# Four of the sixteen x tiles turned by a transposing DMA instead of TensorE, and three steps of the MLP part put at a slot's end

## The chip, the cores and the metric

One core of a Trainium2 chip runs the whole kernel in one launch. The metric is the time of one execution on the device in microseconds (us), the median of several runs.

## The reference

The kernel computes one transformer block on x of 2048 rows by 512 columns, in float32:

```
h  = x + attention(layernorm(x) @ wqkv) @ wo
h2 = h + (relu(layernorm(h) @ w1 + b1) ** 2) @ w2 + b2
```

The attention has 32 heads of 16 columns each. A row looks at 8 positions: itself and those 2, 4, .. 14 rows before it, with softmax over the 8. The MLP is 1792 wide.

## The kernel before

**Tiles.** x is cut in 16 tiles of 128 rows. Matrix products on TensorE need the left operand turned, columns on partitions, so every tile of x (after its layernorm), of the attention's output o and of the normalised h is turned before its product. Each operand is held as a high and a low part in a reduced float format, and a product is three matmul groups, high by high, low by high and high by low, of four 128x512 matmuls each (`mm3`, L228). In the program's names `xh`, `xl` are the parts of x, `oh`, `ol` (or `ohl`) those of o, `w_h`, `w_l`, `big_h`, `big_l` those of weights or h.

**Two ways to turn a tile.** On TensorE (`transposes`, L201): four 128x128 transposes into PSUM (`tr`); ScalarE casts the high part (L152) and VectorE subtracts it for the low part (L155). By DMA: `turn_split` (L616, ScalarE) separates the upper and lower 16 bits of each value into two planes (`pl`), `turn_dma` (L620, SyncE) issues one `DMA_TRANSPOSE`, and `turn_join` (L625, ScalarE) puts the halves together again; casts follow as before. Before the change, all x tiles go by TensorE, and some tiles of o (the set `OV`) and of h (`HV`) by DMA.

**Stages.** The first phases, `first_phase(t0)` for t0 = 4, 6, .. 14, each compute the projections of two tiles, t0 and t0 + 1, in six products (`qkv_of`, tiles alternating, so the second product of a phase is the first that needs tile t0 + 1), and prepare the tiles of the next phase: load (L438), statistics (`x_stats`, L182 to L184 on ScalarE), normalisation (`x_norm`, L196), turn (`x_T`). Results go through PSUM copies (`y`, L523) to DRAM (L500), and the attention loads windows of k, v (L247) and q (L260) back. A phase has twelve half-slots m. `weight_job` (L573) loads and splits one piece of wo or w1. Then come three MLP units u = 0, 1, 2 over four tiles each and a last one, with `wo_product`, the addition of the residual and of b2 (`h_add`, `add_b2` L674 on POOL), and the split of w2 (`split_w2`).

**What sets the order.** The order of the program is written by hand, slot by slot. Steps are put on lists: `at(n, ...)` for the end of the slot n from now, `after(n, ...)` for the same place but behind the attention's steps. At the end of a slot:

```
    def end_slot(pe):
        now["pe"] += pe
        run(due)
        pump()
        run(amid)
        run(late)
        now["slot"] += 1
```

`run(due)` emits what `at` listed, `pump` emits attention steps (dots L339, sums L373, maximum and exponential L390 to L396, weighting L350 on VectorE and ScalarE; additions L407 on POOL) up to a modelled VectorE time, and `run(late)` emits what `after` listed. Every engine works through its instructions in that order and waits at each for what it needs. SyncE issues all DMAs, in order, so a load that waits for VectorE to free its buffer holds the DMAs behind it.

Of the kernel before, what the change touches and what calls it, by code (L numbers as in the profile page):

```python
# [9 lines left out]
F32R = mybir.dt.float32r  # L10
# [6 lines left out]
P = 128  # L17
KB = D // P
FB = F // P
R = 4  # L20
RI = 2
# [17 lines left out]
XT = (9, 11), (7, 8)  # L39
# [19 lines left out]
def block_kernel(ctx, tc, x, wqkv, wo, w1, b1, w2, b2, out):  # L59
# [42 lines left out]
    def row(name, shape=(P, D), dt=F32):  # L102
        return work.tile(list(shape), dt, name=name, tag="row", bufs=ROWS)
# [9 lines left out]
    def at(delta, fn, *a):  # L113
        due.setdefault(now["slot"] + delta, []).append((fn, a))

    def after(delta, fn, *a):
        late.setdefault(now["slot"] + delta, []).append((fn, a))
# [33 lines left out]
    def hi(dst, src):  # L151
        nc.scalar.copy(dst, src)  # L152
# [45 lines left out]
    def transposes(src, banks="tr"):  # L198
        tr = turn[banks].tile("tr").rearrange("p (k c) -> p k c", k=KB)
        for k in range(KB):  # L200
            nc.tensor.transpose(tr[:, k, :], src[:, k * P:(k + 1) * P], ident)  # L201
        now["pe"] += 0.44
        return tr

    def parts(tr, dst):
        n = len(dst)
        return [(dst[i], tr[:, i * KB // n:(i + 1) * KB // n]) for i in range(n)]

    def hi_T(tr, h_dst):
        for d, src in parts(tr, h_dst):  # L210
            hi(d, src)
# [220 lines left out]
    xt, xT = {}, {}  # L432
# [35 lines left out]
    def x_T(t):  # L468
        tr = transposes(xt.pop(t))
        xT[t] = row("xh", (P, KB, P), F32R), row("xl", (P, KB, P), F32R)  # L470
        at(0, hi_T, tr, [xT[t][0]])
        after(0, lo_T, tr, [xT[t][0]], [xT[t][1]])

    ny = [0]

    turn["mm"] = Turn("mm0", "mm1", "acc0", "acc1")
# [90 lines left out]
    jobs = [(wo_h, wo_l, wo, k, 0, D) for k in range(KB)]  # L567
# [37 lines left out]
    planes = {}  # L605
# [4 lines left out]
    def two_planes(a):  # L610
        return a.bitcast(U16).rearrange("p (two n) -> p two n", two=2)

    def turn_split(key, src):

        planes[key] = src, row("pl")
        nc.scalar.copy(two_planes(planes[key][1]), halves_of(src))  # L616
# [6 lines left out]
    def turn_join(key):  # L623
        src, pl = planes[key]
        nc.scalar.copy(halves_of(pl).rearrange("p two n -> p n two"),  # L625
                       two_planes(src).rearrange("p two n -> p n two"))
        planes[key] = pl.rearrange("p (k c) -> p k c", k=KB)
# [55 lines left out]
    def wo_product(t, slots):  # L683
        ps = turn["mm"].tile("wo")
        oh, ol = oT.pop(t)
        mm3(ps, lambda k: oh[:, k, :], lambda k: ol[:, k, :],
            lambda k: wo_h[:, k, :], lambda k: wo_l[:, k, :], lows_last=t in OV)
        for n, (fn, a) in zip(slots, ((h_add, (t, ps)), (h_norm, (t,)), (add_b2, (t,)),
                                      (spill, (t,)))):
            (after if fn in (h_norm, spill) else at)(n + (fn is add_b2), fn, *a)  # L690

# [283 lines left out]
    for n in range(16):  # L977
        gp, t = divmod(n, 4)
# [27 lines left out]

    def first_phase(t0):
        def chores(m):
            if t0 + 3 < 16:
                if m in (0, 2):  # L1010
                    at(0, x_stats, t0 + 2 + m // 2)

                early = t0 == 12
                if m + early in ((4, 6) if t0 == R else (6, 7)):
                    at(0, x_norm, t0 + 2 + (m + early) // 7 if t0 > R else t0 + m // 2)
                if m in XT[early]:
                    x_T(t0 + 2 + XT[early].index(m))
            if t0 + 5 < 16 and m in (6, 9):
                at(0, load_x, t0 + 2 + m // 3)
            if jobs and m % 3 == 0:  # L1020
                at(0, weight_job)
            k = t0 // 2 * 12 - 72 + m
            if k == 19:
                dve(HOLD)
            for t in range(R):
                if k == OT[t]:
                    at(0, load_h, t)
                    o_T(t)
                if t in HV and k == HK[t][0]:
                    at(0, h_split, t)  # L1030
                    after(0, turn_dma, ("h", t))
                if t in HV and k == HK[t][1]:
                    at(0, turn_join, ("h", t))
                if k == WO[t]:
                    wo_product(t, (1, 3, 4, 6))
                    now["pe"] += 2.73
                if k == HT[t]:
                    (at(0, h_parts, t) if t in HV else h_T(t))
            if k in W2:
                at(0, load_w2, W2.index(k))  # L1040

        def half(m):
            end_slot(1.37)
            chores(m)

        for n in range(6):
            chores(2 * n)
            qkv_of(t0 + n % 2, n // 2, lambda: half(2 * n + 1))
            end_slot(1.37)
# [40 lines left out]
    for u in range(R - 1):  # L1090
        now["sub"] = u
        first, end = u == 0, False
        fs = list(range(FB)) if first else [*sorted(place), 12, 13]
        fs += [f for f in range(12) if f not in fs and (u < 2 or f not in ENDS)]
        fs += ENDS if u == 2 else []
        need = [] if first else [f for f in fs if f < 12 and f not in place]
        acc = [psum.tile([P, D], F32, name="acc", tag=tag) for tag in ("acc0", "acc1", "tr0", "tr1")]
        js = range(R)


        todo, halves = {}, {}
        for i in js:
            t = R * (u + 1) + i
            if not end:
                a = i // 2 if u == 2 else 0
                o0 = OP[i] - a - (2 if i >= RI and t in OV else 0)
                if t in OV:
                    turned = [(o0, at, 0, o_split, t), (o0, at if i >= RI else after, i // RI, turn_dma, ("o", t)),
                              (o0 + 2, at, 0, o_join, t)]
                else:  # L1110
                    turned = [(o0, o_T, t)]
                if t in HV:
                    h0 = 11 + i
                    turned += [(h0, midway, 0, h_split, t), (h0, after, 0, turn_dma, ("h", t)),
                               (h0 + 2, at, 0, turn_join, ("h", t))]
                for p, *what in ((LH[i] - a, at, 0, load_h, t), *turned,
                                 (WP[i] - a, wo_product, t, (0, 1, 2 + 3 * a, 3 + 3 * a))):
                    todo.setdefault(p, []).append(what)
                p, h = (HP[i], i % 2) if u < 2 else HL[i]
                if t in HV:  # L1120
                    todo.setdefault(p, []).append((at, 0, h_parts, t))
                else:
                    (todo, halves)[h].setdefault(p, []).append((h_T, t))
            todo.setdefault(UP[i], []).append((at, 0, unspill, R * u + i))
        if u == 2:
            for p, *what in ((12, at, 0, t_load, 0), (12, at, 0, t_load, 1), (13, after, 0, t_sums, 0),
                             (13, after, 0, t_sums, 1), (13, at, 1, t_split, 0),
                             (14, after, 0, t_split, 1)):
                todo.setdefault(p, []).append(what)

        def half(p):
            run(due)
            for fn, *a in halves[p]:
                fn(*a)

        for p in range(FB + LAG):
            more = 0.0
            if p == FB:
                run(due)
                dve(HOLD)  # L1140
            if u < 2 and p == FB - 2:
                dve(HOLD)
            for fn, *a in sorted(todo.get(p, []), key=lambda x: x[0] is wo_product):
                fn(*a)
                more += 2.73 if fn is wo_product else 0.0
            if p < FB:
                mlp1(u, fs[p])
                more += 2.73
                if first:
                    at(0, split_w2, p)  # L1150
                    if p + 1 < FB:
                        load_w2(p + 1)
            q = p - LAG
            if q >= 0:
                f = fs[q]
                mlp2(u, f, acc, js, q == 0, q == FB - 1,
                     (lambda: half(p)) if p in halves else None)
                more += 2.74
                if f < 12 and (need or first and p < FB - LAG):
                    free.append(place.pop(f))  # L1160
                    if need:
                        at(1, fetch, need.pop(0))
            end_slot(more)
        for i in js:
            at(u // 2, finish, R * u + i, acc[i])
# [83 lines left out]
```

## Time and profile before

| | |
|---|---|
| runs | 510.28, 510.4, 510.7 us; median 510.4 |
| profiled execution | 510.82 us, of which the span is 509.0 us |
| TensorE (PE) busy | 498.7 us, 98% |
| VectorE (DVE) busy | 380.8 us, 75% |
| ScalarE (ACT) busy | 304.7 us, 60% |
| GpSimd (POOL) busy | 357.2 us, 70% |
| granted TensorE clock | 1.00 |

In the profile's lines PE is TensorE's matmuls, PEld its weight loads (beside them), DVE VectorE, ACT ScalarE, SP SyncE, which issues the DMAs. A timeline row has start and duration in us, engine, line, operation, output and inputs by the program's names, shapes, count, and in brackets the idle time before it with what ended that. Matmuls are pipelined: rows of one line overlap, and the time of a group is read from start to start. Of a group of rows the three numbers after the count are minimum, median and maximum in ns. "to landing" is the time from a DMA's issue until its data is there.

### The profile page before, as it was taken

What the parts mean: (1) busy time and instruction counts of PE and PEld (TensorE: products, weight loads), DVE (VectorE), ACT (ScalarE), POOL (GpSimd) and SP (SyncE); (2) the same over time, 40 slices, a digit from 0 to 9 for tenths busy, and PEclk for the clock granted to TensorE, in tenths of its full rate; (3) what the DMA queues carried; (4) which work ended last, traced back from release to release, by engine and by line L of the source; (5) the groups of instructions that cost most, each with busy time, mean ns of one, the idle gap of its engine ahead of it and who ended that gap; (6) DMA issues with size and microseconds to landing.
All of it is one profiled execution on the core that took longest, in us unless ns stands there. A gap on an engine that the chain in (4) does not pass through costs nothing.

```text
span 509.0 us, 7539 instructions
## 1 busy us (share of the span) xinstructions
PE 498.7 (98%) x2422; PEld 420.7 (83%) x2422; DVE 380.8 (75%) x512; ACT 304.7 (60%) x558; POOL 357.2 (70%) x434
## 2 busy tenths in 40 slices
PE   8999999999999999999999999989999999999997
PEld 7999778888888888887788888768888888998986
DVE  6469899999989799979879997898973137832233
ACT  4625677768346757386564566754556947566541
POOL 5714689986685899969777876976897465685610
PEclk9999999999999999999999999999999999999999
DMA  8577899989798898669676874967662372444212
GB/s 265 162 238 204 229 300 297 262 271 317 219 220 254 277 283 253 231 176 245 193 249 199 215 195 130 263 221 231 210 160 67 102 217 82 166 127 142 64 42 82
DMA packets 109359, 102.61 MB, mean 202 GB/s; under 512 B 29448, under 2 KB 77832, under 8 KB 109320
## 3 DMA queue, kind: packets, MB, share of 16 engines
q1 hardware_dynamic: 108376, 101.61, 68.0%
q10 hardware_dynamic: 944, 0.52, 0.3%
q8 instruction: 19, 0.31, 0.3%
q14 instruction: 20, 0.16, 0.1%
HBM read 72.65 MB, written 24.25 MB: 190 GB/s over the span
## 4 chain that ended last, share of the span: by engine, by line
PE 41%; POOL 5%; ACT 4%; DMA 3%; DVE 1%; issue 1%; SPq 0%; POOLq 0%; DVEq 0%; ACTq 0%
PE acc L895 19%; PE mm L228 12%; PE mm L818 6%; PE wo L228 3%; POOL pr L407 2%; DMA o<-pl 1%; DMA hn<-pl 1%; POOL h L674 1%; DMA h<-h_d 1%; ACT pl L625 1%; ACT pl L616 1%; ACT hn L196 1%; DVE pr L350 0%; POOL o L407 0%; PE tr L201 0%
## 5 line engine op out<-in xcount | busy, mean ns | idle before, releaser
L407 POOL TENSOR_TENSOR pr<-pr 128x512 f32<-128x512 f32 (+1 forms) x128 | 133.7, 1044 | 34.6 <-DVE pr L350 29.1
L228 PE MATMUL mm<-big_l,w_h 128*128 128x512 f32 x336 | 88.5, 390 | 1.6 <-DVE big_l L155 0.9
L350 DVE TENSOR_TENSOR pr<-ex,v 128x1024 f32<-128x1024 f32 x64 | 78.1, 1221 | 13.1 <-POOL o L407 8.1
L339 DVE TENSOR_TENSOR pr<-qp,k 128x1024 f32<-128x1024 f32 x64 | 76.8, 1200 | 8.8 <-ACT qp L268 6.9
L373 DVE TENSOR_REDUCE ex<-pr 128x64 f32<-128x1024 f32 x64 | 78.5, 1226 | 1.9
L228 PEld LDWEIGHTS mm<-big_l,w_h 128*128 128x128 f32 x336 | 62.9, 188 | 15.4 <-issue 1.3
L155 POOL TENSOR_TENSOR rl<-r,rh 128x512 fp32r<-128x512 f32 x42 | 55.5, 1322 | 20.2 <-ACT rh L152 20.2
L228 PE MATMUL mm<-big_l,xh 128*128 128x512 f32 (+1 forms) x208 | 55.8, 378 | 0.0
L228 PE MATMUL mm<-big_h,xh 128*128 128x512 f32 (+1 forms) x208 | 53.9, 380 | 1.3 <-ACT xh L152 1.0
L228 PE MATMUL mm<-big_h,xl 128*128 128x512 f32 (+1 forms) x208 | 52.7, 375 | 0.7 <-DVE xl L155 0.7
L895 PE MATMUL acc<-big_l,rh 128*128 128x512 f32 x190 | 52.2, 390 | 0.0
L895 PE MATMUL acc<-big_h,rh 128*128 128x512 f32 x190 | 52.1, 391 | 0.0
L895 PE MATMUL acc<-big_h,rl 128*128 128x512 f32 x190 | 51.7, 389 | 0.0
L228 PEld LDWEIGHTS mm<-big_h,xh 128*128 128x128 f32 x208 | 37.6, 188 | 8.9 <-ACT xh L152 2.6
L228 PE MATMUL mm<-big_l,w_l 128*128 128x512 f32 x168 | 44.9, 389 | 0.0
L228 PEld LDWEIGHTS mm<-big_h,xl 128*128 128x128 f32 x208 | 38.2, 188 | 6.9 <-DVE xl L155 1.1
L871 ACT ACTIVATE r<-mm,b_sb 128x512 f32<-128x512 f32 x42 | 28.7, 684 | 22.5 <-PE mm L228 20.7
L895 PEld LDWEIGHTS acc<-big_h,rl 128*128 128x128 f32 x190 | 35.7, 188 | 7.4
L895 PEld LDWEIGHTS acc<-big_l,rh 128*128 128x128 f32 x190 | 35.5, 188 | 7.4
L228 PEld LDWEIGHTS mm<-big_l,xh 128*128 128x128 f32 x208 | 37.5, 188 | 4.9
L895 PEld LDWEIGHTS acc<-big_h,rh 128*128 128x128 f32 x190 | 34.9, 188 | 6.7
L228 PEld LDWEIGHTS mm<-big_l,w_l 128*128 128x128 f32 x168 | 31.5, 188 | 6.6
(167 smaller groups left out, 918.7 us busy)
## 6 DMA issues: line engine op xcount, KB each, us to landing
k<-qkv_d SPq DMA_DIRECT2D x48, 288.0 KB, 3.0
v<-qkv_d SPq DMA_DIRECT2D x48, 288.0 KB, 4.1
qkv_d<-y SPq DMA_DIRECT2D x18, 512.0 KB, 4.7
big_l<-w2l_d SPq DMA_DIRECT2D x24, 256.0 KB, 3.0
xt<-in_A_x_dram SPq DMA_DIRECT2D x16, 256.0 KB, 4.2
q<-qkv_d SPq DMA_DIRECT2D x32, 128.0 KB, 3.8
h<-in_A_x_dram SPq DMA_DIRECT2D x16, 256.0 KB, 4.2
h_d<-h SPq DMA_DIRECT2D x16, 256.0 KB, 3.2
```

Of the source, the lines that this page charges most:

```text
L155: eng.tensor_tensor(out=dst, in0=src, in1=h, op=ALU.subtract)
L196: nc.scalar.activation(dst, src, AF.Identity, scale=rs[:, 0:1], bias=rs[:, 1:2])
L228: nc.tensor.matmul(ps, l(k), r(k), start=(n == 0), stop=(n == 3 * KB - 1))
L339: nc.vector.tensor_tensor(out=pr.rearrange("p i w h d -> p i w (h d)"), in0=qps["now"][:, j % 2].unsqueeze(2).to_broadcast([P, RI, W, GC]) ...
L350: nc.vector.tensor_tensor(out=p2, in1=vwin, op=ALU.mult, in0=e1[:, :, :, j * GH:(j + 1) * GH].unsqueeze(4).to_broadcast([P, RI, W, GH, DH]))
L373: nc.vector.tensor_reduce(out=lf[:, :, :, j * GH:(j + 1) * GH], in_=pr, axis=X, op=ALU.add)
L407: nc.gpsimd.tensor_tensor(out=dst, in0=p2[:, :, :w], in1=p2[:, :, w:2 * w], op=ALU.add)
L616: nc.scalar.copy(two_planes(planes[key][1]), halves_of(src))
L625: nc.scalar.copy(halves_of(pl).rearrange("p two n -> p n two"), two_planes(src).rearrange("p two n -> p n two"))
L818: nc.tensor.matmul(ps, sta[y][:, k], mov[x][:, k], start=(first and q == 0), stop=(last and q == len(terms) - 1), skip_group_check=True)
L871: nc.scalar.activation(r, ps, AF.Relu, bias=b1_sb[:, f:f + 1])
L895: nc.tensor.matmul(acc[j], l[:, j * P:(j + 1) * P], w[f], start=(first and n < len(js)), stop=(last and n >= len(terms) - len(js)))
```

## The change

Tiles 9, 11, 13 and 15, each the second of its phase's pair, are turned by DMA. `x_split` is listed at half-slot 8 of the phase before (7 for tile 15), with its DMA at the end of that slot; `x_join` stands at half-slot 0 of the tile's own phase, ahead of the next tiles' statistics (tile 15: at half-slot 11 of the phase before its own). `x_T` stays for the first tile of a pair, and for both tiles of the first of these phases. The weight jobs' half-slots change in the phases. In the MLP part the addition of b2, the split of w2, and the split and DMA of the third attention tile of a unit (`i == RI`) move from `at` to `after`.

```
+    def x_split(t):
+        turn_split(("x", t), xt.pop(t))
+
+    def x_join(t):
+        turn_join(("x", t))
+        tr = planes.pop(("x", t))
+        xT[t] = row("xh", (P, KB, P), F32R), row("xl", (P, KB, P), F32R)
+        hi_T(tr, [xT[t][0]])
+        after(0, lo_T, tr, [xT[t][0]], [xT[t][1]])
...
-            (after if fn in (h_norm, spill) else at)(n + (fn is add_b2), fn, *a)
+            (at if fn is h_add else after)(n + (fn is add_b2), fn, *a)
...
+            if m == 0 and 6 < t0 < 14:
+                at(0, x_join, t0 + 1)
+            if m == 11 and early:
+                at(0, x_join, 15)
...
-                if m in XT[early]:
+                if m in XT[early][:1 + (t0 == R)]:
                     x_T(t0 + 2 + XT[early].index(m))
+                if t0 > R and m == 8 - early:
+                    at(0, x_split, t0 + 3)
+                    after(0, turn_dma, ("x", t0 + 3))
...
-            if jobs and m % 3 == 0:
+            if jobs and m in ((0, 3, 6, 9) if t0 < 8 else (0, 4, 8) if t0 < 14 else (0, 3, 5)):
                 at(0, weight_job)
...
-                    turned = [(o0, at, 0, o_split, t), (o0, at if i >= RI else after, i // RI, turn_dma, ("o", t)),
+                    turned = [(o0, after if i == RI else at, 0, o_split, t),
+                              (o0, at if i > RI else after, i // (RI + 1), turn_dma, ("o", t)),
                               (o0 + 2, at, 0, o_join, t)]
...
-                    at(0, split_w2, p)
+                    after(0, split_w2, p)
```

On SyncE at the end of the phase t0 = 6, where tile 9 is turned (`xt` are x tiles, `qkv_d` the stored projections, `y` their copies, `raw` pieces of weights, `pl` the planes), the rows of before and then of after:

```order
54 L500 DMA qkv_d<-y_90 128x8x128
55 L247 DMA k<-qkv_d 128x704
56 L260 DMA q<-qkv_d 128x2x128
57 L438 DMA xt<-in_A_x_dram 128x512
58 L573 DMA raw<-in_B_w_dram 128x448
```
```order
54 L510 DMA qkv_d<-y_90 128x8x128
55 L247 DMA k<-qkv_d 128x704
56 L260 DMA q<-qkv_d 128x2x128
57 L630 DMA_TRANSPOSE xt<-pl 128x8x128
58 L438 DMA xt<-in_A_x_dram 128x512
59 L583 DMA raw<-in_B_w_dram 128x448
```

The transpose stands behind the k and q loads, and the xt load and the weight load move one place back. The lines of the changed kernel are 10 higher here.

On ScalarE at the turn of that phase to t0 = 8 (L196 the normalisation, L152 casts, L182 to L184 statistics, L268 the copy of q for the attention, L396 the exponential, `y` a result's copy out of PSUM), before and after:

```order
79 L152 CAST w_h<-raw 128x448
80 L152 CAST xh<-tr 128x512
81 L523 COPY y_90<-mm 128x8x64
82 L152 CAST xh<-tr 128x512
83 L152 CAST w_h<-raw 128x448
84 L523 COPY y_90<-mm 128x8x64
85 L182 ACTIVATE scrap,nm<-xt 128x512
86 L183 ACTIVATE nm<-nm 128x1
87 L184 ACTIVATE scrap,sq<-xt,nm 128x512
88 L268 COPY qp<-q 128x256
89 L523 COPY y_90<-mm 128x8x64
```
```order
78 L626 COPY pl<-xt 128x1024
79 L396 ACTIVATE ex<-ex 128x128
80 L152 CAST w_h<-raw 128x448
81 L152 CAST xh<-tr 128x512
82 L533 COPY y_90<-mm 128x8x64
83 L152 CAST w_h<-raw 128x448
84 L533 COPY y_90<-mm 128x8x64
85 L635 COPY pl<-xt 128x1024
86 L152 CAST xh<-pl 128x512
87 L182 ACTIVATE scrap,nm<-xt 128x512
88 L183 ACTIVATE nm<-nm 128x1
89 L184 ACTIVATE scrap,sq<-xt,nm 128x512
```

The second cast of x from PSUM is gone; the split stands ahead of an exponential, and the join with its cast stands between a result's copy and the statistics of the next tiles.

On ScalarE in the MLP unit u = 0, around the third attention tile's split (L871, L872 the squared relu and `rh` its high part, `hn` the normalised h), before and after:

```order
230 L152 CAST rh<-r 128x512
231 L616 COPY pl<-o 128x1024
232 L152 CAST big_h<-raw_2434 128x512
233 L396 ACTIVATE ex<-ex 128x256
234 L196 ACTIVATE hn<-h,rs 128x512
235 L871 ACTIVATE r<-mm,b_sb 128x512
```
```order
237 L152 CAST rh<-r 128x512
238 L268 COPY qp<-q 128x256
239 L396 ACTIVATE ex<-ex 128x256
240 L196 ACTIVATE hn<-h,rs 128x512
241 L626 COPY pl<-o 128x1024
242 L152 CAST big_h<-raw_2422 128x512
243 L881 ACTIVATE r<-mm,b_sb 128x512
```

The split of o and that of w2 stand behind the exponential and the normalisation, where they stood ahead of them.

More of the change, by code (lines that the diff above doesn't have):

```diff
@@ L1008, in chores @@
         def chores(m):
+            early = t0 == 12
+            if m == 0 and 6 < t0 < 14:
+                at(0, x_join, t0 + 1)
+            if m == 11 and early:
+                at(0, x_join, 15)
             if t0 + 3 < 16:
@@ L1011, in chores @@
                     at(0, x_stats, t0 + 2 + m // 2)
-                early = t0 == 12
                 if m + early in ((4, 6) if t0 == R else (6, 7)):
                     at(0, x_norm, t0 + 2 + (m + early) // 7 if t0 > R else t0 + m // 2)
-                if m in XT[early]:
+                if m in XT[early][:1 + (t0 == R)]:
                     x_T(t0 + 2 + XT[early].index(m))
+                if t0 > R and m == 8 - early:
+                    at(0, x_split, t0 + 3)
+                    after(0, turn_dma, ("x", t0 + 3))
             if t0 + 5 < 16 and m in (6, 9):
                 at(0, load_x, t0 + 2 + m // 3)
-            if jobs and m % 3 == 0:
+            if jobs and m in ((0, 3, 6, 9) if t0 < 8 else (0, 4, 8) if t0 < 14 else (0, 3, 5)):
                 at(0, weight_job)
```

## The prediction

> **What bounds the kernel now.** I read the page first (span, busy shares), then the busy time by stretches through the stage in which the x tiles are turned, then the timelines of TensorE, SyncE and ScalarE around the four places that lose transposes, and last the idle times of TensorE in the MLP part.
>
> ```profile
> span 509.0 us, 7539 instructions
> PE 498.7 (98%) x2422; PEld 420.7 (83%) x2422; DVE 380.8 (75%) x512; ACT 304.7 (60%) x558; POOL 357.2 (70%) x434
> DMA  8577899989798898669676874967662372444212
> 75.00:90.00 15.00, 15.00 (x72) 12.40 (x71) 14.47 (x24) 10.85 (x27) 13.86 (x19) 1.00 0.98 302
> 90.00:105.00 15.00, 15.00 (x72) 12.40 (x71) 14.53 (x20) 10.62 (x25) 13.41 (x19) 1.00 0.92 274
> 105.00:120.00 15.00, 15.00 (x72) 12.40 (x71) 13.95 (x18) 10.25 (x23) 13.86 (x20) 1.00 0.88 279
> ```
>
> TensorE is busy for 498.7 of 509.0 us. The row of digits is the busy share of the DMA engines in 40 slices of 12.7 us, in tenths: it is highest up to slice 16 (203 us) and lower after it. In the stretches of 15 us (columns: PE, PEld, DVE, ACT, POOL busy, granted clock, share of the DMA engines, GB/s) it is busy the whole time at clock 1.00, so a TensorE instruction taken out there shortens the span by its time, and a TensorE wait put in there lengthens it. Two other columns bear on the change: DVE is 14 of 15 us busy, so what holds DVE is not caught up within a phase, and the DMA engines are 88 to 98% busy, so a transfer put there queues.
>
> **The transposes that go.** Sixteen TensorE transposes are removed, four for each of tiles 9, 11, 13 and 15.
>
> ```profile
> 77.40 1.09 PE L228 MATMUL mm<-big_h,xh 128*128 128x512 f32 x4
> 78.79 0.60 PE L201 MATMUL tr<-ident,xt 128*128 128x128 f32 x4
> 80.62 1.07 PE L228 MATMUL mm<-big_h,xh 128*128 128x512 f32 x4
> 83.34 1.07 PE L228 MATMUL mm<-big_h,xh 128*128 128x512 f32 x4
> ```
>
> The product that holds tile 9's transposes (78.79) runs from 77.40 to 80.62, 3.22 us; the next, without, from 80.62 to 83.34, 2.72 us. One tile's transposes so cost 0.50 us of TensorE, and four tiles 4 x 0.50 = **-2.0 us**. [...]
>
> **Where the turned tile now comes from.** In the new path ScalarE splits the normalised tile into two planes, SyncE issues one transposing DMA, ScalarE joins the planes and casts the high part, and VectorE forms the low part. Each step stands in order on its engine: behind the join on ScalarE are the statistics, the query copy and the next result's copy; behind the low part on VectorE is the attention. The pieces that the trace has:
>
> ```profile
> 78.92 0.47 SPq L260 DMA_DIRECT2D q<-qkv_d  x1
> 79.48 0.46 SPq L438 DMA_DIRECT2D xt<-in_A_x_dram  x1
> 85.14 0.63 ACT L182 ACTIVATE scrap<-xt 128x512 f32<-128x512 f32 x1 [0.39 <-DMA xt<-in_A_x_dram]
> L625 ACT COPY pl<-o x12: 1163/1174/1178, 199.0 to 405.5; 128x1024 uint16<-128x1024 uint16 x12
> L152 ACT CAST oh<-pl x9: 620/621/628, 200.2 to 406.8; 128x512 fp32r<-128x512 f32 x9
> L620 SPq DMA_TRANSPOSE o<-pl x12: 1237/1242/3462, 195.4 to 395.8; - x12
> DMA to landing us min/median/max: 3.6/4.4/7.0
> ```
>
> *Tile 9.* On SyncE the new transpose stands where this xt load stands at 79.48, directly behind the query load of 78.92, so it can go no earlier than about 79.4 whatever ScalarE does: the key load ahead of it waits for VectorE to free its buffer. The xt load issued there landed at 85.14 (ScalarE's statistics were released by it then), 5.7 us after issue; the transposes of the trace, issued where DMA is less busy, landed after 3.6 to 7.0 us. I take 85.1, the same place in the queue and the same bytes (128x512 in float32, two 128x512 planes of 16 bits). Then join 1.17 and cast 0.62 give the high part at 85.14 + 1.79 = 86.93. TensorE wants it at the first product of tile 9, which was at 83.34 and would be at 82.84 without the 0.50 us of transposes. The stall is 86.93 - 82.84 = **4.1 us**. Bounds: a landing 3.6 us after 79.4 gives 83.0 + 1.79 = 84.8 and 2.0 us; 7.0 us gives 86.4 + 1.79 = 88.2 and 5.4 us. Nothing gets ahead meanwhile: ScalarE stands at the join until 85.1, VectorE at the low part until 86.9, SyncE's loads wait for VectorE's buffers. So the 4.1 us are paid in full and the stages behind move by about the same.
>
> ```profile
> 95.41 0.32 SPq L247 DMA_DIRECT2D v<-qkv_d  x1
> 95.82 0.38 SPq L438 DMA_DIRECT2D xt<-in_A_x_dram  x1
> DMA to landing us min/median/max: 4.2/4.2/4.2
> 100.62 1.07 PE L228 MATMUL mm<-big_h,xh 128*128 128x512 f32 x4
> 110.12 0.43 SPq L500 DMA_DIRECT2D qkv_d<-y  x1
> 117.91 1.07 PE L228 MATMUL mm<-big_h,xh 128*128 128x512 f32 x4
> 129.13 0.33 SPq L247 DMA_DIRECT2D v<-qkv_d  x1
> 145.26 1.07 PE L228 MATMUL mm<-big_h,xh 128*128 128x512 f32 x4
> ```
>
> *Tile 11* (times as before, the earlier stall left out, since all move together). Its transpose stands behind the value load of 95.41, where an xt load is issued at 95.82 and lands 4.2 us later (the landing shown is that load's alone). 95.8 + 4.2 + 1.79 = 101.8 against a need at 100.62 - 0.50 = 100.12: **1.7 us** (3.6 us: 1.1; 7.0 us: 4.5). *Tile 13.* Issue behind the store of 110.12, at 110.6; even with 5.0 us to landing the high part is there at 117.4, and it is wanted at 117.91 - 0.50 = 117.41: 0 (7.0 us: 2.0). *Tile 15.* Issued behind the load of 129.13, joined four half-slots later, wanted around 145.26: 0 at any landing of the trace. Sum of stalls **5.8 us**, between 3.1 and 11.9.
>
> [...]
>
> The other edits of this stage cost nothing that I can find: X in phases where ScalarE is 10 to 11 of 15 us busy, and as many weight jobs as before remain, spread otherwise over the slots.
>
> **The MLP part.** Here TensorE does wait a little:
>
> ```profile
> 234.22 1.20 PE L228 MATMUL mm<-big_l,w_h 128*128 128x512 f32 x4 [0.69 <-ACT r L871]
> 250.81 0.66 PE L201 MATMUL tr<-ident,hn 128*128 128x128 f32 x4 [0.69 <-ACT hn L196]
> 321.39 1.20 PE L228 MATMUL wo<-wo_h,ohl 128*128 128x512 f32 x4 [0.54 <-ACT ohl L152]
> 332.25 1.20 PE L228 MATMUL wo<-wo_h,ol 128*128 128x512 f32 x4 [0.44 <-DVE ol L155]
> 343.47 1.15 PE L228 MATMUL mm<-big_l,w_h 128*128 128x512 f32 x4 [0.93 <-DVE big_l L155]
> 218.44 1.05 ACT L616 COPY pl<-o 128x1024 uint16<-128x1024 uint16 x1 [7.07 <-POOL o L407]
> 219.40 0.61 ACT L152 CAST big_h<-raw 128x512 fp32r<-128x512 f32 x1
> 220.31 0.42 DVE L362 TENSOR_REDUCE sm<-ex 128x32 f32<-128x256 f32 x1 [3.10 <-ACT ex L396]
> 309.15 1.05 ACT L616 COPY pl<-o 128x1024 uint16<-128x1024 uint16 x1 [7.46 <-POOL o L407]
> 310.50 0.42 DVE L362 TENSOR_REDUCE sm<-ex 128x32 f32<-128x256 f32 x1 [2.76 <-ACT ex L396]
> 224.25 1.25 SPq L620 DMA_TRANSPOSE o<-pl  x1
> 230.42 1.32 POOL L674 TENSOR_TENSOR h<-h,b_sb 128x512 f32<-128x512 f32 x1
> 231.67 1.78 POOL L155 TENSOR_TENSOR rl<-r,rh 128x512 fp32r<-128x512 f32 x1
> ```
>
> The five waits are 0.69 + 0.69 + 0.54 + 0.44 + 0.93 = 3.29 us. The third attention split holds ScalarE 7 us waiting for POOL, and the exponential queued behind it comes late for VectorE by 3.10 and 2.76 us. Put behind the exponential and the normalisation, it holds neither; its DMA, at 224.25 though the planes were ready about 219.5, moves ahead of a key load that waits. The bias addition (1.32 us) moves behind the low part of r, which comes that much earlier. I count the three waits directly on these chains (234.22, 321.39, 332.25: 1.67 us) as gone, and half of the other two (0.81): **-2.5 us**, from 0 (the turned tile or another result is next by as much) to -3.3. The weight split at a slot's end leaves ScalarE's later work free sooner and I count nothing for it. If the idle time of ScalarE that covers it is gone, its cast (0.61 us at 219.40) would come into the wait for r once per weight block.
>
> **The sum.** -2.0 + 5.8 - 2.5 = +1.3 us. The profiled execution took 510.82 us, 509.0 of it span; it would become 512.1. The runs shown have a median of 510.4, 0.4 below it, so the time is 510.4 + 1.3 = **511.7 us**. What a measurement here can tell from no change is about 0.2%, 1.0 us: 511.7 is just beyond it.
>
> **Rivals.** *A, early landings, faster.* If the transposes of tiles 9 and 11 land at the fast end, 3.6 us, the stalls are 2.0 + 1.1 = 3.1, and with all 3.3 us of the MLP waits gone it is -2.0 + 3.1 - 3.3 = -2.2: 508.2 us. It turns faster by over 1.0 us where the stalls are under 3.5 with 2.5 recovered. For it: the fast transposes of the trace. Against: those ran with DMA less busy, while here it is 98%, and the load in that very place took 5.7. *B, late landings, slower by more.* At 7.0 us for tiles 9 and 11 the stalls are 5.4 + 4.5 = 9.9; with 2.0 recovered, -2.0 + 9.9 - 2.0 = +5.9: 516.3. For it: the slowest transpose of the trace took that where DMA was less busy than here; against: the load's 4.2 at tile 11. *C, nothing recovered.* The stalls of the forecast come, and in the MLP the waits stay, since the attention's end there is set by POOL, which ended both splits' waits: -2.0 + 5.8 = +3.8: 514.2. *D, a wash.* The transposes wait for nothing and hide, and the MLP waits stay but for one: it needs landings under 2 us at tile 9, which no row shows, or stalls near 4.5 with 2.5 recovered: 510.4.
>
> **How the numbers follow.** The forecast's own case (stalls 4.5 to 7, half or more recovered) has 0.45, of which about 0.10 falls within 0.2%; A 0.18, all faster; B 0.17; C 0.13; D 0.07, same. Faster 0.19, same 0.17, slower 0.64. The range runs from A, 508.2, to somewhat over B, 517.0 (B with 1.3 recovered), which leaves about one in ten outside on either side.
>
> **What would show it.** In the new trace: no transposes of xt near 78.8, 96.1, 113.4, 130.2; a TensorE wait on the high part of x in front of tile 9's first product of about 4 us and in front of tile 11's of about 2, none for 13 and 15; ScalarE's join released by the DMA there; VectorE idle for the high part at the same places. In the MLP, the 3.10 and 2.76 us idle times of VectorE gone and TensorE's waits under 1 us in sum. A TensorE that runs through tile 9's start without a wait would make the forecast wrong, and so would a wait for tile 13.

## The result, and the profile after

The changed kernel takes 521.88 us (median of four runs, 521.43 to 523.0) against 510.34 before: a ratio of 1.0231, 95% interval [1.0211, 1.0251]. It is 11.5 us slower. The forecast was 511.7 us in a range of 508.2 to 517.0: the direction was right and the size was not.

The page of the changed kernel, its span, busy times and DMA row, and the same three stretches as before:

```profile
span 519.9 us, 7521 instructions
PE 502.3 (97%) x2406; PEld 421.8 (81%) x2406; DVE 375.1 (72%) x512; ACT 312.8 (60%) x566; POOL 355.5 (68%) x434
DMA  9677989789798888958577766785754373255212
75.00:90.00 15.00, 11.25 (x42) 8.63 (x41) 12.20 (x18) 9.55 (x22) 10.50 (x15) 0.82 1.00 283
90.00:105.00 15.00, 15.00 (x66) 12.33 (x65) 11.80 (x17) 8.25 (x18) 11.71 (x15) 0.95 0.70 193
105.00:120.00 15.00, 13.95 (x63) 11.17 (x63) 11.86 (x17) 12.64 (x27) 10.24 (x15) 1.00 0.81 247
```

Two things stand out. TensorE waits in the stretches where it never did, and although it has 16 instructions fewer it is busy 3.6 us longer: in the first stretch the granted clock is 0.82 in the mean. The rows of TensorE around the four tiles and in the MLP part of the changed kernel:

```profile
79.25 1.07 PE L228 MATMUL mm<-big_h,xh 128*128 128x512 f32 x4
86.04 2.07 PE L228 MATMUL mm<-big_h,xh 128*128 128x512 f32 x4 [3.75 <-ACT xh L152]
87.91 1.91 PE L228 MATMUL mm<-big_l,xh 128*128 128x512 f32 x4
89.62 1.91 PE L228 MATMUL mm<-big_h,xl 128*128 128x512 f32 x4
91.33 1.17 PE L228 MATMUL mm<-big_h,xh 128*128 128x512 f32 x4
106.72 1.21 PE L228 MATMUL mm<-big_h,xh 128*128 128x512 f32 x4 [1.05 <-ACT xh L152]
124.53 1.19 PE L228 MATMUL mm<-big_h,xh 128*128 128x512 f32 x4 [0.66 <-ACT xh L152]
...
240.55 1.20 PE L228 MATMUL wo<-wo_h,ohl 128*128 128x512 f32 x4 [2.15 <-ACT ohl L152]
241.59 1.82 PE L228 MATMUL wo<-wo_l,ohl 128*128 128x512 f32 x4
243.82 1.77 PE L228 MATMUL wo<-wo_h,ohl 128*128 128x512 f32 x4 [0.41 <-DVE ohl L155]
245.42 1.09 PE L228 MATMUL mm<-big_l,w_h 128*128 128x512 f32 x4
```

Tile 9's product starts 3.75 us late and then takes 91.33 - 86.04 = 5.29 us where one takes 2.72, since every group of four matmuls takes nearly twice its time (2.07, 1.91 and 1.91 us against 1.07; the granted clock is 0.50 from 86 to 90 us). The same happens after the wait of 2.15 us at 240.55 (0.50 from 242 to 244 us): that product takes 4.87 us, 0.41 of it a second wait.

TensorE's first turn of h in the MLP part, before and after:

```profile
157.51 0.60 PE L201 MATMUL tr<-ident,hn 128*128 128x128 f32 x4
163.81 0.60 PE L201 MATMUL tr<-ident,hn 128*128 128x128 f32 x4
```

So TensorE leaves the first phases 6.3 us late: -0.9 from smaller waits in the first 70 us, -2.0 from the transposes, +5.5 from the three waits, +2.6 from the slow product, and 1.1 that I can't assign row by row. In the MLP part, from this row to the last matmul (it starts at 505.40 before and 516.56 after), 4.9 us more are lost: the waits there add up to 6.3 us where they were 3.3, and the slow product at 240 us costs 1.7. The remainder of the span gives 0.3 back.

ScalarE and SyncE at tile 9, the steps of which the forecast's stall was made:

```profile
77.78 0.32 SPq L247 DMA_DIRECT2D k<-qkv_d  x1
78.16 0.48 SPq L260 DMA_DIRECT2D q<-qkv_d  x1
78.73 1.52 SPq L630 DMA_TRANSPOSE xt<-pl  x1
84.12 1.16 ACT L635 COPY pl<-xt 128x1024 uint16<-128x1024 uint16 x1 [4.08 <-DMA xt<-pl]
85.37 0.62 ACT L152 CAST xh<-pl 128x512 fp32r<-128x512 f32 x1
```

The transpose stands behind the two loads, lands 5.4 us after its issue, and join and cast follow at once, as forecast.

### The profile page after: what moved, and what is told of

Read it like the earlier page. It is cut to its first block, busy times and chain, and to the rows that moved or that the text cites. A ratio compares the mean times of both kernels' runs of the same rounds, so it can differ in the third digit from the quotient of the medians.

```text
span 519.9 us, 7521 instructions
## 1 busy us (share of the span) xinstructions
PE 502.3 (97%) x2406; PEld 421.8 (81%) x2406; DVE 375.1 (72%) x512; ACT 312.8 (60%) x566; POOL 355.5 (68%) x434
## 4 chain that ended last, share of the span: by engine, by line
PE 37%; POOL 8%; ACT 6%; DVE 5%; issue 3%; POOLq 0%; DVEq 0%; ACTq 0%
PE acc L905 16%; PE mm L228 11%; PE mm L828 6%; POOL pr L407 4%; PE wo L228 3%; DVE pr L350 2%; ACT pl L626 1%; POOL rl L155 1%; POOL o L407 1%; ACT r L881 1%; ACT pl L635 1%; ACT r L882 1%; ACT hn L196 1%; DVE ol L155 1%; POOL h L684 0%
## 5 line engine op out<-in xcount | busy, mean ns | idle before, releaser
L350 DVE TENSOR_TENSOR pr<-ex,v 128x1024 f32<-128x1024 f32 x64 | 78.0, 1220 | 14.3 <-POOL o L407 9.9
L228 PE MATMUL mm<-big_h,xh 128*128 128x512 f32 (+1 forms) x208 | 55.0, 386 | 6.2 <-ACT xh L152 6.1
```

Of the source, the lines that this page charges most:

```text
L228: nc.tensor.matmul(ps, l(k), r(k), start=(n == 0), stop=(n == 3 * KB - 1))
L350: nc.vector.tensor_tensor(out=p2, in1=vwin, op=ALU.mult, in0=e1[:, :, :, j * GH:(j + 1) * GH].unsqueeze(4).to_broadcast([P, RI, W, GH, DH]))
```

## The experiments

The questions were whether the MLP loss is the price of the late attention (theory 1) or of the MLP edits (theory 2), and what the slow clock costs.

**All x tiles on TensorE again** (the cadence of the weight jobs and the MLP edits stay):

```
-            if m == 0 and 6 < t0 < 14:
-                at(0, x_join, t0 + 1)
-            if m == 11 and early:
-                at(0, x_join, 15)
...
-                if m in XT[early][:1 + (t0 == R)]:
+                if m in XT[early]:
...
-                if t0 > R and m == 8 - early:
-                    at(0, x_split, t0 + 3)
-                    after(0, turn_dma, ("x", t0 + 3))
```

> All x tiles are turned on TensorE again; the new weight cadence and the MLP edits stay. Theory 1 (the MLP part is slow after the change because the attention comes out of the first phases late; its own edits are harmless): TensorE's waits in the MLP are back to 3.3 us or less in sum, the clock is 1.00 throughout, and the time is 508 to 511 us. Theory 2 (the MLP edits themselves cost the 4.9 us): the stalls at tiles 9, 11, 13 and the slow clock there are gone, but the waits near 240 us stay, and the time is 510.4 + 5 = 515 us.

Measured: 509.07 us, ratio to before 0.9987 [0.9971, 1.0002]. The MLP edits with the new cadence cost nothing; whether they gain 0.1% can't be told. Theory 2 falls.

**The MLP edits undone**, the turned tiles kept (the three lines of the diff on `add_b2`, the third split and `split_w2` as before):

> The MLP edits are undone (bias addition, third split and its DMA, weight split at their old places); the turned x tiles and the cadence stay. Theory 1: the late attention still meets the MLP part: 520 to 525 us. Theory 2: the MLP part is as before, the loss is that of the first phases alone (+6.3 us in the trace): 516 to 517 us.

Measured: 521.09 us, 1.0233 [1.0197, 1.0269]. Most of the loss in the MLP part stays without the edits: in the trace TensorE leaves the first phases at 164.53, 7.0 us late, and the MLP part is 2.9 us longer than before, where it was 4.9 with the edits. Nothing here speaks against theory 1 yet.

**Tile 9 alone on TensorE:**

```
-            if m == 0 and 6 < t0 < 14:
+            if m == 0 and 8 < t0 < 14:
...
-                if m in XT[early][:1 + (t0 == R)]:
+                if m in XT[early][:1 + (t0 <= 6)]:
...
-                if t0 > R and m == 8 - early:
+                if t0 > 6 and m == 8 - early:
```

> Tile 9 alone is turned on TensorE again. Both theories: the 3.75 us stall and the slow clock behind it (2.9 us) go, 0.5 us of transposes come back, so TensorE leaves the first phases about 6.1 us earlier. Theory 1: with the attention less late, the MLP loss of 4.9 us shrinks to 2 or less: 511 to 513 us. Theory 2: it stays: 515 to 516 us.

Measured: 512.94 us, 1.006 [1.0042, 1.0078], 8.9 us less than the changed kernel. The time came where theory 1 had it, but not in its way. TensorE leaves the first phases at 160.80, 3.0 us earlier than in the changed kernel and not 6.1, since tile 11 now waits 2.00 us and its product runs slow (the granted clock is 0.997 in the mean of the span, 1.00 before). The MLP loss is gone altogether: that part is 0.4 us shorter than before, though TensorE comes to it 3.3 us late.

**TensorE kept busy in the wait:**

```
+            if t0 == 8 and n == 1:
+                keep_busy(16)
             qkv_of(t0 + n % 2, n // 2, lambda: half(2 * n + 1))
```

> Sixteen matmuls that nothing uses (3.6 us of TensorE at full clock) stand between the first product of tile 8 and the first of tile 9, in the wait. If the clock falls because TensorE stands idle, the granted clock stays 1.00 from 84 to 92 us, tile 9's first product takes 2.7 us and not 5.3, and the time is 521.9 - 2.6 = 519.3 us or lower. If it falls for another reason (DMA load, power at that place), the time stays near 522 us.

Measured: 523.3 us, 1.0261 [1.0236, 1.0286]. TensorE's rows of this kernel, and stretches of its time:

```profile
82.94 3.79 PE L1020 MATMUL tr<-big_h 128*128 128x512 f32 x16
87.20 1.20 PE L228 MATMUL mm<-big_h,xh 128*128 128x512 f32 x4 [0.47 <-ACT xh L152]
88.24 1.08 PE L228 MATMUL mm<-big_l,xh 128*128 128x512 f32 x4
107.82 1.20 PE L228 MATMUL mm<-big_h,xh 128*128 128x512 f32 x4 [3.51 <-ACT xh L152]
84.00:88.00 4.00, 3.53 (x16) 2.60 (x15) 1.46 (x3) 2.61 (x5) 1.95 (x3) 1.00 1.05 336
88.00:92.00 4.00, 4.00 (x19) 3.31 (x18) 2.93 (x6) 3.90 (x13) 1.42 (x5) 1.00 0.58 186
```

Half of the expectation came: the clock stays at 1.00 from 84 to 92 us, where the changed kernel has 0.58 from 84 to 88 and 0.56 from 88 to 92, and tile 9's product takes 2.86 us (the next one starts at 90.06). With the DMA engines as busy as in the changed kernel (a share of 1.05 here, 1.02 there, from 84 to 88 us) and a wait of 0.47 us in place of 3.75, it was TensorE's standing idle that took the clock down here. The time doesn't follow: tile 11's wait grows from 1.05 to 3.51 us. What tile 11 waits for is its own chain, a transpose behind a value load that waits for VectorE (1.3 us in the changed kernel, for L390), then the landing (5.1 us there), join and cast; that chain had lost its time at tile 9 and takes no notice of how fast TensorE ran in between. The slow product was hidden under a wait to come.

**The x tiles' DMA one step earlier** (`at` in place of `after`, so that it stands ahead of the key or value load):

> The x tiles' transposing DMAs are listed with at, so that each stands ahead of the key or value load that it stood behind: tile 9's can start when its planes are ready, about 76.1 us, where it started at 78.7. Theory 1 (the wait is the transfer's start and landing, and what VectorE loses in it is not regained): about 2.5 us earlier at tile 9 and up to as much at tile 11, less lag of the attention and most of the MLP loss gone: 512 to 516 us. Theory 3 (DMA is saturated there and the landing moves little whatever the issue): 520 to 522 us.

Measured: 516.29 us, 1.0131 [1.0104, 1.0159], 5.6 us less than the changed kernel. The start of the transfer matters; theory 3 falls. But its MLP part still shows the 2.15 us wait, and TensorE leaves the first phases 0.3 us ahead of before. The lateness was gone and the loss in the MLP part, 5.7 us, was not.

**Normalisation and split three half-slots earlier:**

```
+                elif m in (4, 6):
+                    at(0, x_norm, t0 + 3 if m == 4 else t0 + 2)
...
-                if t0 > R and m == 8 - early:
+                if t0 > R and m == (7 if early else 5):
```

> In the phases of t0 = 6, 8 and 10 the second tile is normalised at half-slot 4 (was 7) and split at 5 (was 8), its DMA behind it, so that the planes are under way some 4 to 5 us earlier. Theory 1: tiles 9, 11 and 13 are in place when TensorE wants them; no wait there, clock 1.00, no MLP loss; the 2.0 us of transposes then show: 507 to 509 us, below the kernel with all tiles on TensorE (509.07). Theory 3: the waits shrink but stay over 1 us each: 512 or more.

Measured: 516.05 us, 1.0117 [1.0091, 1.0143]. The stalls on the turned tiles are gone, TensorE leaves the first phases 1.4 us ahead, and 5.1 us are lost in the MLP part all the same.

**VectorE held 4.1 us** in the kernel with all x tiles on TensorE:

```
+            if t0 == 8 and m == 0:
+                for i in range(6):
+                    nc.vector.bn_stats(small.tile([P, 6], F32, name="hold"), b2_sb)
```

> The kernel of e1 (all x tiles on TensorE), with six statistics instructions that nothing uses (0.69 us each, 4.1 us of VectorE) put in at the start of the phase of t0 = 8. Theory 1 (VectorE is the second bound, lateness of the attention is paid in the MLP): TensorE does not wait in the first phases but the time grows by 2 to 4 us, in waits near 163, 230 to 245 or 320 us: 511 to 513 us. Rival (VectorE has the slack that its 72% busy share suggests): 509 to 509.5 us.

Measured: 509.88 us, 1.0012 [0.9999, 1.0025], 0.8 more than without. The rival was nearly right. In the traces TensorE leaves the first phases 1.6 us later than without the hold (158.22 against 156.59), and the MLP part is as long in both. So theory 1 falls from two sides: lateness without the change costs nothing in the MLP part, and the change without lateness (the two runs before this one) costs 5 to 6 us there.

**Tiles 13 and 15 alone by DMA** (9 and 11 on TensorE):

> Tiles 9 and 11 on TensorE, 13 and 15 by DMA. Tile 13's wait was 0.66 us behind two late phases. Theory 1: with nothing late ahead of it tile 13's wait is 0 to 0.7 us, 1.0 us of transposes is saved, VectorE's idle time there is under 1.7 us: 508.5 to 510.5 us. If tile 13's wait does not depend on the lateness before it, VectorE idles 1.7 us there as before and the time is 510 to 512 us.

Measured: 513.31 us, 1.0067 [1.0038, 1.0095], but ten runs lie between 509.4 and 516.5 and the profiled one at 509.41. One kernel, with one order, so spreads over 7 us, and this settles nothing.

**The order.** What all kernels with the MLP loss share is that four calls of `transposes` are gone, and `transposes` does one thing more than its four instructions: `now["pe"] += 0.44`. The pump emits the attention's steps until modelled VectorE time has caught up with modelled TensorE time. Four calls fewer leave that time 1.76 us lower, and every step of the attention behind them may be emitted a slot later, to the end of the kernel. Theory 4 is that this order is the loss. It need not grow call by call: with three calls gone (tile 9 on TensorE) the profiled run showed no loss. It was tried from both sides: the model's time put back without the transposes, and taken away with them.

```
+            if t0 > R and t0 + 3 < 16 and m == (8 if early else 11):
+                now["pe"] += 0.44
```

> The changed kernel, with 0.44 us put back to the modelled TensorE time at the half-slot where each of the four removed transposes stood; no instruction is added, and VectorE's order in the MLP becomes that of e1. Theory 4 (the MLP loss comes from the order: without the transposes the model holds TensorE 1.76 us earlier, so the attention's steps are emitted later against TensorE's): the stalls and the lag of the first phases stay as they are (about +6 us), the 5 us of the MLP go: 514.5 to 517 us. Theory 1 (the loss comes from the late attention in time): 520 us or more.

Measured: 518.5 us, 1.0169 [1.015, 1.0188], above the range of theory 4 and below that of theory 1. Of the 4.9 us of the MLP part nothing is left, 0.8 are gained there; but the first phases are 2 us slower than expected, since tile 13 waits 3.23 us in place of tile 11, and its product is a second slow one (the granted clock is 0.50 from 126 to 128 us). TensorE's row of it:

```profile
125.21 2.08 PE L228 MATMUL mm<-big_h,xh 128*128 128x512 f32 x4 [3.23 <-ACT xh L152]
```

> The kernel of e1 (all x tiles on TensorE, no DMA turn) with 0.44 us taken from the modelled TensorE time at each of the four transposes, so that VectorE's order in the MLP becomes that of the changed kernel. Theory 4: the MLP waits of the changed kernel (near 233 to 241, 252 to 262, 325 to 333, 399 to 406 us) appear although nothing is late: 513 to 515 us. Theory 1: 509 to 510 us, as e1.

This is the kernel with all x tiles on TensorE and `-= 0.44` at the same place: no DMA turn, nothing late. Measured: 515.03 us, 1.0101 [1.0079, 1.0122], 6.0 us more than the same instructions in the other order. In its trace TensorE leaves the first phases at 155.70, 0.9 us ahead of the kernel with all x tiles on TensorE, and its waits in the MLP part add up to 8.2 us where they were 2.5. VectorE's order in the MLP part is that of the changed kernel. VectorE's rows in the MLP unit u = 0, in the kernel with all x tiles on TensorE and then in this one:

```
235 L155 TENSOR_TENSOR ol<-pl,oh 128x512
236 L350 TENSOR_TENSOR pr<-ex,v 128x1024
237 L671 TENSOR_TENSOR h<-wo,h 128x512
238 L163 BN_STATS st<-h 128x6
239 L164 BN_AGGR mv<-st 128x2
240 L390 TENSOR_REDUCE mx<-ex 128x32
```
```
236 L671 TENSOR_TENSOR h<-wo,h 128x512
237 L163 BN_STATS st<-h 128x6
238 L164 BN_AGGR mv<-st 128x2
239 L350 TENSOR_TENSOR pr<-ex,v 128x1024
240 L390 TENSOR_REDUCE mx<-ex 128x32
```

The weighting (L350) that completes the third tile's o stood ahead of `h_add` and stands behind it. Timelines of the first kernel (VectorE, POOL, TensorE) and then of the second (VectorE, POOL, ScalarE, TensorE):

```profile
213.21 1.21 DVE L350 TENSOR_TENSOR pr<-ex,v 128x1024 f32<-128x1024 f32 x1
220.40 0.46 POOL L407 TENSOR_TENSOR o<-pr 128x128 f32<-128x128 f32 x1
231.76 1.07 PE L228 MATMUL wo<-wo_h,ohl 128*128 128x512 f32 x4
```
```profile
212.60 1.21 DVE L350 TENSOR_TENSOR pr<-ex,v 128x1024 f32<-128x1024 f32 x1
213.89 2.12 POOL L407 TENSOR_TENSOR pr<-pr 128x512 f32<-128x512 f32 x2 [1.76 <-DVE pr L350]
216.53 1.21 DVE L350 TENSOR_TENSOR pr<-ex,v 128x1024 f32<-128x1024 f32 x1
222.52 0.46 POOL L407 TENSOR_TENSOR o<-pr 128x128 f32<-128x128 f32 x1
223.02 1.05 ACT L626 COPY pl<-o 128x1024 uint16<-128x1024 uint16 x1 [3.36 <-POOL o L407]
231.42 1.16 ACT L635 COPY pl<-o 128x1024 uint16<-128x1024 uint16 x1
230.06 1.07 PE L905 MATMUL acc<-big_h,rl 128*128 128x512 f32 x4
233.28 1.20 PE L228 MATMUL wo<-wo_h,ohl 128*128 128x512 f32 x4 [2.15 <-ACT ohl L152]
```

The chain of this wait begins one weighting earlier, since other weightings come later here too: the one at 212.60 stands at 210.15 in the first kernel. POOL's additions waited 1.76 us for it, and POOL's rows show no further wait up to o at 222.52, 2.1 us later than in the first kernel. ScalarE stood at the split until then, and its rows show no wait from there to the join at 231.42 (229.61 in the first kernel); the transfer itself, issued behind that split, had landed by then, since the join shows no wait. So TensorE waits for ScalarE's queue, not for the DMA.

The changed kernel shows the same chain about 7.3 us later, down to the 2.15 us at 240.55:

```profile
221.17 2.11 POOL L407 TENSOR_TENSOR pr<-pr 128x512 f32<-128x512 f32 x2 [1.76 <-DVE pr L350]
230.29 1.05 ACT L626 COPY pl<-o 128x1024 uint16<-128x1024 uint16 x1 [3.37 <-POOL o L407]
```

Theory 4 is shown for the loss in the MLP part, 4.9 of the 11.5 us; the rows explain one of its waits, and the others were not followed to their start. The rest of the 11.5 us lies in the first phases.

**Early split and the model's time together** (the kernel with normalisation and split three half-slots earlier, plus the two lines above):

> The kernel of e6 (second tile normalised and split three half-slots earlier) with the same 0.44 us put back four times. Theory 4: nothing of either loss is left; e6's trace leaves the first phases 1.4 us ahead of the kernel before and lost 5.2 us after it, so 516.05 - 5 to 6.5 = 509.5 to 511 us by the medians, or 507 to 509 us by the profiled runs. Theory 1 was e6's own forecast and did not come; if the order is not the cause it stays at 514 to 516 us.

Measured: 511.07 us, 1.0019 [1.0006, 1.0032], 5.0 us below the same kernel without the two lines. What is left of the loss is a new wait, three times: TensorE's waits in this kernel (in total, times, longest):

```profile
PE tr L201 <- ACT xt L196: 4.3, 3, 1.7
```

The first tile of each pair is normalised behind the second one's split on ScalarE, and its transposes wait: 4.3 us against 2.0 gained.

**The first tile's normalisation ahead of the split:**

```
-                elif m in (4, 6):
+                elif m in (4, 5):
```

> The kernel of e10 with the first tile's normalisation at half-slot 5 (was 6), ahead of the split. In e6 TensorE waited 1.54 us at 75.7 us for that normalisation, which stood behind the split and a copy on ScalarE. With it ahead, that wait goes and the second tile's planes are at most 0.8 us later: 1 to 1.5 us faster than e10, 508 to 509.5 us by the median.

Measured: 512.63 us, 1.0052 [1.0036, 1.0068]: a miss. That wait is gone and another has come. ScalarE, TensorE, and stretches of time in this kernel:

```profile
80.81 0.57 ACT L152 CAST w_h<-raw 128x448 fp32r<-128x448 f32 x1 [3.17 <-DMA raw<-in_B_w_dram]
81.77 1.16 ACT L635 COPY pl<-xt 128x1024 uint16<-128x1024 uint16 x1
83.69 1.65 PE L228 MATMUL mm<-big_h,xh 128*128 128x512 f32 x3 [2.21 <-ACT xh L152]
82.00:84.00 2.00, 0.31 (x1) 0.31 (x2) 1.32 (x2) 1.91 (x3) 1.92 (x3) 0.82 1.11 380
84.00:86.00 2.00, 2.00 (x6) 1.54 (x6) 1.97 (x4) 1.94 (x7) 1.75 (x4) 0.50 1.01 390
```

The join stands behind a weight cast that waits 3.17 us for its load, in a slice of the page (76.6 to 89.4 us) in which the DMA engines are busy for 90% or more. No version with turned x tiles beat the one that keeps them all on TensorE, and that one can't be told from the kernel before.

## Why the prediction was wrong, point by point

The sum was +1.3 us, and the span grew by 10.9. Of the 9.6 us between, 7.4 lie in the MLP part (-2.5 forecast, +4.9 measured) and 2.5 in the first phases (+3.8 forecast, +6.3 measured); the rest of the span gives 0.3 back.

- **Transposes, -2.0 us: right in size, wrong as the whole.** TensorE's part came as worked out. The step that failed is that this term counted the call's four instructions and put at nothing its entry in the model that sets the order. A sign of it stood in ScalarE's rows of the change: a copy of q (L268) of the attention ahead of the exponential, where none stood before. The runs put that entry at +6.0 us (515.03 against 509.07).
- **Stalls, 4.1 + 1.7 + 0 = 5.8 us: right in sum, in part by luck.** Measured 3.75 + 1.05 + 0.66 = 5.46. At tile 9 the stand-in, the load at the same place of the queue, was good: 5.7 us to landing taken, 5.4 measured. Tile 11's 1.7 rested on "all move together", and they didn't: its landing took 5.1 us for 4.2, and the slow product held TensorE back by 2.6 us, so that 1.05 us of wait was left. With the clock kept up tile 11 waited 3.51 us. Tile 13's 0 came as 0.66, which the prediction had named as a sign of being wrong.
- **What follows from a stall: missed.** The sum had the wait alone. Behind it TensorE ran one product at about half the clock (0.50 from 86 to 90 us), +2.6 us. In the first phases this was no addition of its own, since the run that kept the clock up waited as much later; in the MLP part it added 1.7.
- **"Nothing gets ahead meanwhile": nearly right.** VectorE stood still at tile 9 and tile 11, as said, and tile 11's readiness moved with VectorE and not with TensorE.
- **MLP part, -2.5 us: wrong in sign in the changed kernel, +4.9.** The reasoning on the third split could only hold with the order kept. With it kept (all x tiles on TensorE) VectorE's idle times of 3.10 and 2.76 us are gone from the trace as forecast, but the traces with that order and these edits give only 0.8 to 1.9 us from the first phases' end to the last matmul, and the time of the kernel with these edits alone (509.07) does not stand clear of the one before: the term was too large as well.
- **Rivals.** By its number B (516.3) was nearest, but for landings of 7.0 us, which did not come (5.4 and 5.1). By its mechanism C was (the MLP waits stay), and it gave them for POOL's sake; that they would grow was in none of them.

## What to carry to other kernels

Where a planner's modelled time sets the order, taking an instruction out also takes its entry out of the model; separate the two with a run that changes only the entry, before explaining lateness in time. A wait that a full engine shows can belong to a chain that is late on other engines: here, filling the wait moved the loss to the next tile, whose wait grew from 1.05 to 3.51 us. When a transfer must be early, count what stands ahead of its consumers on every engine, since each repair here made another of them the last (in the last run the join stood behind a cast that waited 3.17 us).

## What the runs showed of the hardware

The granted clock of TensorE fell to 0.50 after some of its waits, and their length alone does not tell which. It fell after 3.75 us (tile 9, 0.50 from 86 to 90 us), 3.23 us (the run with the model's time put back, tile 13, 0.50 from 126 to 128 us) and 2.21 us (the last run, 0.50 from 84 to 86 us). A wait of 2.15 us brought it down in the changed kernel (0.50 from 242 to 244 us) and in the run with the DMA one step earlier (0.50 from 235 to 237 us) and not in the run with the order alone (1.00 from 230 to 240 us), and it did not fall after 3.51 us in the run that filled the first wait:

```profile
106.00:108.00 2.00, 0.18 (x1) 0.18 (x2) 0.20 (x1) 1.91 (x3) 0.00 (x0) 1.00 0.86 222
108.00:110.00 2.00, 2.00 (x10) 1.62 (x11) 1.91 (x3) 1.94 (x7) 0.35 (x2) 1.00 1.12 363
```

No run here tells why some waits brought it down and others did not.
